# Windowed attention with one tile shape for everything but the score products, and score banks shared by two engines

## The chip, the cores and the metric

The kernel runs on one core of a Trainium2 chip. The metric is the device time of one execution in microseconds (us); the time before is the median of three runs. A change of 0.2% is about what a measurement of this kernel can tell from none.

## The reference

```python
# x: (1, 224, 224, 96), wqkv: (96, 288), wo: (96, 96), all bf16; sw = 8, C = 96, C2 = 48
qkv = einsum('bhwc,cd->bhwd', x, wqkv);  q, k, v = split(qkv, 3)
# first half of the channels: 28 horizontal stripes of 8 x 224 = 1792 tokens
ah = softmax(qh @ kh.T * C2**-0.5);   oh = ah @ vh
# second half: 28 vertical stripes of 224 x 8 = 1792 tokens
av = softmax(qv @ kv.T * C2**-0.5);   ov = av @ vv
return concat(oh, ov) @ wo
```

So there are 56 independent attention windows, each of 1792 queries by 1792 keys with 48 channels, and a projection in front and behind. Nearly all work is the scores (QK), their exponential, and the product of the exponentials with V (PV).

## The kernel before, in words

Windows go in pairs `P` = 0 to 27 (14 horizontal pairs, then 14 vertical ones); the two windows of a pair are called `w` = 0 and 1 and use partitions 0 to 63 and 64 to 127. A pair's queries are cut into four chunks `CH` of 512, 512, 512 and 256, its keys into 14 tiles of 128. A *unit* is one chunk by one key tile (two key tiles in the 256-wide chunk), for both windows: 49 units a pair, 1372 in all.

One unit's QK is two matmuls of 512 columns, one a window, with 48 rows by 128 columns of weights (four of 256 columns in the short chunk): the array is then used as two tiles of 64 rows by 128 columns, which run side by side. One unit's PV is two matmuls with 128 rows by 49 columns of weights (48 channels of V and a column of ones that sums the exponentials): two tiles of 128 rows by 64 columns, side by side again.

Units are of two sorts. `a_units` (42 a pair, 1176 in all): QK writes two PSUM banks, ScalarE takes the exponential of both in one ACTIVATE (L672) into `PT`, PV reads it. `d_units` (7 a pair, 196 in all, numbers `ND`, `NDL`): VectorE approximates the exponential as a sum of `J` = 4 terms. It scales the scores (L698, one instruction a window, `Y_sb`), makes four integer images of them (L710, `L_sb`), and TensorE adds four PVs with four scaled copies of V (`VD_sb`, made by GpSimd at L495).

Around this lie the *fills*, products that prepare the next pair and finish the last: transposes of x (L409, L422; weights of 96 columns over 112 or 128 rows), the projections to K and Q (L437; 96 rows by 64 columns, two side by side), to V (L481; 96 rows by 128 columns), and the output projection (`fin`: L519 for horizontal pairs, 49 by 64; L550 for vertical ones, 49 by 128). VectorE moves each result out of PSUM.

PSUM has eight banks. Banks 0 to 3 are two pairs (`a_sets`) for the ACTIVATEs. Banks 4 to 7 (`banks`) are shared by the score halves of `d_units`, the fills and the open PV sums (at most two, `live`).

The order of work on each engine is not written by hand. `Planner` simulates five engines with a cost per operation (`dur`) and a delay between engines (`SLACK`), and takes from a set of streams, each with a priority, what can start first; among what can start within 0.03 us, the lowest priority number. On TensorE these are `pe_qa`, `pe_qd`, `pe_pd`, `pe_pa`, `pe_fin`, `pe_fill` = 0 to 5. The result is a fixed order with semaphore waits, which every engine follows: an instruction that waits holds all behind it on that engine. `soft` dependences only pace the plan. The SyncE queue issues all DMAs.

Of the kernel before, what the change touches and what calls it, by code (L numbers as in the profile page):

```python
# [45 lines left out]
ND = 2  # L46
NDL = 1


class Op:  # L50
    __slots__ = ("eng", "dur", "fn", "deps", "soft", "alloc", "then", "idx", "end", "wait", "tok", "dma")

    def __init__(s, eng, dur, fn, deps=(), soft=(), alloc=(), then=None, dma=None):
        s.eng, s.dur, s.fn, s.deps, s.soft, s.alloc, s.then = eng, dur, fn, list(deps), list(soft), list(alloc), then
        s.idx = s.end = s.wait = None
        s.tok, s.dma = {}, dma


class Pool:
# [6 lines left out]
    def peek(s, when):  # L66
        best = None
        for k in s.slots:
            f = s.free_by[k]
            if f is None or any(o.end is None for o in f):  # L70
                continue
            t = max([when(o) for o in f], default=0.0)
            if best is None or t < best[0]:
                best = (t, k)
        return best

    def take(s, k):
        f = s.free_by[k]
        s.free_by[k] = None
        return f  # L80
# [5 lines left out]
SLACK = {  # L86
    ("act", "pe"): 0.10, ("pe", "act"): 0.15, ("dve", "pe"): 0.4, ("pe", "dve"): 0.35, ("dve", "dve"): 0.05,
    ("pool", "pe"): 1.5, ("dve", "pool"): 0.3, ("pool", "dve"): 0.8, ("pool", "pool"): 0.1, ("pe", "pe"): 0.0,
    ("dve", "sp"): 0.2, ("pool", "sp"): 0.2, ("pe", "sp"): 0.2, ("sp", "pe"): 1.0, ("sp", "dve"): 1.0,
    ("sp", "pool"): 1.0, ("act", "dve"): 0.2, ("dve", "act"): 0.2, ("act", "act"): 0.0, ("pe", "pool"): 0.3,  # L90
    ("sp", "sp"): 0.0, ("act", "sp"): 0.2,
}


class Planner:
    def __init__(s, sems):
        s.sems = sems
        s.t = {e: 0.0 for e in ("pe", "act", "dve", "pool", "sp")}
        s.n = {e: 0 for e in s.t}
        s.out = {e: [] for e in s.t}  # L100
        s.streams = {e: [] for e in s.t}
        s.dma_tot = {}

    def stream(s, eng, prio):
        q = deque()
        s.streams[eng].append((prio, q))
        return q

    def when(s, o, eng):
        return o.end + SLACK.get((o.eng, eng), 0.3)  # L110

    def ready(s, op):
        t = 0.0
        for d in op.deps + op.soft:
            if d.end is None:
                return None
            t = max(t, s.when(d, op.eng))
        for pool, _ in op.alloc:
            b = pool.peek(lambda o: s.when(o, op.eng))
            if b is None:  # L120
                return None
            t = max(t, b[0])
        return t

    def place(s, op, t):
        deps = list(op.deps)
        for pool, name in op.alloc:
            k = pool.peek(lambda o: s.when(o, op.eng))[1]
            deps += pool.take(k)
            op.tok[name] = k  # L130
        e = op.eng
        op.end = t + op.dur
        if op.dma is not None:
# [6 lines left out]
            s.t[e] = t + 0.06  # L140
        else:
# [4 lines left out]
            s.t[e] = op.end  # L146
        if op.then:
            op.then(op)

    def run(s):  # L150
        while True:
            best = None
            for e, streams in s.streams.items():
                cands = []
                for prio, q in streams:
                    if q:
                        r = s.ready(q[0])
                        if r is not None:
                            cands.append((max(r, s.t[e]), prio, q))
                if not cands:  # L160
                    continue
                m = min(c[0] for c in cands)
                c = min((c for c in cands if c[0] <= m + 0.03), key=lambda c: c[1])
# [5 lines left out]
        left = {e: [len(q) for _, q in st] for e, st in s.streams.items() if any(q for _, q in st)}  # L169
        assert not left, left  # L170


def bass_standalone__window_attn_cswin__vision_kernel(
# [11 lines left out]
    CP = C2 + 2  # L185
# [9 lines left out]
    FS, VS = 5, 10  # L195
    scale = float(C2) ** -0.5
    A128 = scale * log2(2.718281828459045) * 128.0
    DKT = max(ND, 2 * NDL)
    NPT, NY, NL = 6, 3, 3
    LEAD, SPACE = 5, 4  # L200

    es = ExitStack()
    with es:
# [3 lines left out]
        w_sb = sb("w_sb", [C, 6, 64], BF16)  # L207
        woh = sb("woh", [128, C + 1], BF16)
        wov = sb("wov", [128, C + 1], BF16)
# [6 lines left out]
        xT_sb = [sb(f"xT_sb{i}", [C, 2, NTOK], BF16) for i in range(2)]  # L216
# [3 lines left out]
        VD_sb = [sb(f"VD_sb{i}", [128, J, 2, max(DKT, 1), CP], BF16) for i in range(2)]  # L220
# [9 lines left out]
        rc = [sb(f"rc{i}", [128, FS], FP32) for i in range(4)]  # L230
        tmp = [sb(f"tmp{i}", [128, FS, C], FP32) for i in range(4)]
        ps = es.enter_context(nc.psum_tensor("ps", [128, 8 * 512], FP32))

        def bank(i):
            return ps[:, i * 512:(i + 1) * 512]

# [10 lines left out]
        pe_qa, pe_qd, pe_pd, pe_pa, pe_fin, pe_fill = (pl.stream("pe", i) for i in range(6))  # L247
# [8 lines left out]
        rcs, tmps = Pool(range(4)), Pool(range(4))  # L256

        def first(eng, dur, fn, deps=()):
            op = Op(eng, dur, fn, deps)
            q_first[eng].append(op)  # L260
            return op

# [5 lines left out]
        first("dve", 0.15, lambda e: e.memset(woh[:], 0.0))  # L268
        o_wov0 = first("dve", 0.15, lambda e: e.memset(wov[:], 0.0))
# [4 lines left out]
        o_ps0 = first("dve", 1.8, lambda e: e.memset(ps[:, 4 * 512:8 * 512], 0.0))  # L274
        for b in range(2):
            o_v1 = first("dve", 0.1, lambda e, b=b: e.memset(V_sb[b][:, :, :, C2:CP], 1.0))
        for k in banks.slots:
            banks.free(k, [o_ps0])
        for i in range(8):
            first("pe", 0.43, lambda e, i=i: e.matmul(bank(i % 4)[:, :], lhsT=warm[:, 0:128], rhs=warm[:, :],  # L280
                                                      start=True, stop=True), [o_warm])
# [9 lines left out]
        def load(P, stream):  # L291
            b = P % 2
            for w in range(2):
                src = x_flat[(2 * P + w) * NTOK:(2 * P + w + 1) * NTOK, :].rearrange("(k p) c -> p k c", p=TH) if is_h[P] else None
                for hf in range(2):
# [7 lines left out]
                    for i, (dst, s_) in enumerate(todo):  # L303
                        op = Op("sp", 2.5, lambda e, dst=dst, s_=s_: e.dma_start(dst, s_),  # L304
# [6 lines left out]
        op_w0 = Op("sp", 2.5, lambda e: e.dma_start(w_sb[:, :, 0:C2], wqkv.rearrange("c (s d) -> c s d", s=6)), [o_w0], dma=(s_w0, 0))  # L311
        q_first["sp"].insert(1, op_w0)
        load(1, q_first["sp"])
        for dst, r0 in ((woh, 0), (wov, C2)):
            for p0 in (0, 64):
                op_w = Op("sp", 2.5, lambda e, dst=dst, r0=r0, p0=p0: e.dma_start(dst[p0:p0 + C2, 0:C], wo[r0:r0 + C2, :]),
                          [o_wov0], dma=(s_w, 0))
                q_first["sp"].append(op_w)
        for dst in (woh, wov):
            for p0 in (C2, 64 + C2):  # L320
                op_w = Op("sp", 2.5, lambda e, dst=dst, p0=p0: e.dma_start(dst[p0:p0 + 1, C:C + 1], one_sb[0:1, 0:1]),
                          [o_one], dma=(s_w, 0))
                q_first["sp"].append(op_w)
# [33 lines left out]

# [3 lines left out]
        def fill(pe_dur, pe_fn, pe_deps, evs, soft=(), stream=None):  # L361

            def freed(op):
                banks.free(p.tok["b"], [op])
            p = Op("pe", pe_dur, lambda e: pe_fn(e, bank(p.tok["b"])), pe_deps, soft, [(banks, "b")])
            ops = []
            prev = p
            for k, (eng, dur, fn, deps, reads, st, alloc, then) in enumerate(evs):
                op = Op(eng, dur, None, [prev] + list(deps), [], alloc)
                op.fn = lambda e, fn=fn, op=op: fn(e, bank(p.tok["b"]), op)  # L370
                ops.append(op)
                op.then = then
# [4 lines left out]
            def both(op):  # L377
                freed(op)
# [11 lines left out]
        def prep(P, pace=None, startup=False):  # L390
# [12 lines left out]
            for w in range(2):  # L403
                for hf in range(2):
                    if is_h[P]:
                        def pe_fn(e, bk, w=w, hf=hf):
                            bkb = bk.bitcast(BF16)
                            for j in range(FTH):
                                ins = e.transpose(bkb[0:C, j * TH:(j + 1) * TH], x_sb[b][0:TH, w, hf * FTH + j, :], ident[0:TH, 0:TH])  # L409
                            return ins  # L410

                        def ev_fn(e, bk, op, w=w, hf=hf):
                            src = bk.bitcast(BF16)[0:C, 0:FTH * TH].rearrange("c (r bc dw) -> c r bc dw", r=RPF, dw=8)
                            dst = xT_sb[b][:, w, :].rearrange("c (bc r dw) -> c r bc dw", r=SW, dw=8)[:, hf * RPF:(hf + 1) * RPF, :, :]
                            return e.tensor_copy(dst, src)  # L415
                    else:
                        ks = list(range(8 * hf, min(NKT, 8 * hf + 8)))

                        def pe_fn(e, bk, w=w, ks=ks):
                            bkb = bk.bitcast(BF16)  # L420
                            for j, k in enumerate(ks):
                                ins = e.transpose(bkb[0:C, j * 128:(j + 1) * 128], x_sb[b][:, w, k, :], ident[:])  # L422
                            return ins

                        def ev_fn(e, bk, op, w=w, ks=ks):
                            return e.tensor_copy(xT_sb[b][:, w, ks[0] * 128:(ks[-1] + 1) * 128], bk.bitcast(BF16)[0:C, 0:len(ks) * 128])  # L426
                    p, ops = fill(0.65, pe_fn, [x_op[(P, w, hf)], o_ident],
                                  [("dve", 0.62, ev_fn, xt_war, True, dve_ev, [], None)], soft() + xt_war)
# [4 lines left out]
            for kind in "kq":  # L433
                for c, (q0, qs) in enumerate(CH):
# [5 lines left out]
                    if kind == "q":  # L440
# [4 lines left out]
                        else:  # L445
                            def ev_fn(e, bk, op, q0=q0, qs=qs):
                                return e.tensor_copy(QT_sb[b][:, q0:q0 + qs], bk[:, 0:qs])  # L447
                            evs = [("dve", 0.63, ev_fn, qk_war, True, dve_ev, [], None)]
                    else:
# [3 lines left out]
                        evs = [("dve", 0.72, ev_fn, qk_war, True, dve_ev, [], None)]  # L453
                        if c == NCH - 1:
# [359 lines left out]
```

## Time and profile before

| | |
|---|---|
| median of 3 runs | 1202.9 us (1201.15 to 1203.32) |
| span of the profiled execution | 1199.9 us |
| TensorE, matmuls (PE) | 1177.9 us busy, 10872 matmuls |
| VectorE (DVE) | 980.0 us busy |
| ScalarE (ACT) | 1135.3 us busy |
| GpSimd (POOL) | 195.4 us busy |
| granted TensorE clock | 0.995 over the span |

The profiled execution's own time is not listed apart from its span; the span runs from its first to its last instruction, 3.0 us below the median of the runs. PE is the row of matmuls and PEld that of weight loads, which overlap them. The ends of matmuls are modelled, so PE's busy share tells little; the distance from start to start tells more. A group "x2352 | 460.2, 386 | 9.6" has 2352 instructions, 460.2 us in which at least one ran, 386 ns for one, and 9.6 us in which the engine stood idle just before one. The chain that ended last, read in order of time, gives for each stretch of one line on TensorE the time until the next stretch starts.

### The profile page before, as it was taken

The page shows a single profiled execution, that of the slowest core. Times are in us where ns is not written, and L with a number is a line of the kernel's source. Part 1 is how long each engine was busy: PE and PEld are TensorE (multiplying, and loading weights), DVE is VectorE, ACT ScalarE, POOL GpSimd, SP SyncE. Part 2 cuts the span into 40 slices and gives each one's busy share as a digit, 9 for nine tenths or more (in the row PEclk, how much of TensorE's full clock was granted, in tenths as well). Part 3 has the DMA queues.
Part 4 walks back from the last instruction along what each step waited for, and adds up shares of the span by engine and source line. Part 5 has one row for each costly group of instructions (what it writes and reads, how often), then busy time and mean ns, then how long its engine had stood idle before and what let it go on. Part 6 is the DMA issues. An engine that isn't in the chain of part 4 may idle for free.

```text
span 1199.9 us, 26677 instructions
## 1 busy us (share of the span) xinstructions
PE 1177.9 (98%) x10872; PEld 441.8 (37%) x10872; DVE 980.0 (82%) x2331; ACT 1135.3 (95%) x1182; POOL 195.4 (16%) x256
## 2 busy tenths in 40 slices
PE   8999999999999999999999999999999999999996
PEld 3333333333333333333333333333333333333332
DVE  7877887888888788788789888887888888888884
ACT  6999999999999999999999999999999999999997
POOL 0100100110010010011003212222222232222221
PEclk8999999999999999999999999999999999999998
DMA  3110110011011001001002211111211221121001
GB/s 73 25 24 1 24 25 18 7 24 24 2 24 24 11 15 24 10 16 25 15 12 37 38 33 35 31 29 36 36 33 34 37 36 33 34 38 21 18 18 24
DMA packets 164946, 30.74 MB, mean 26 GB/s; under 512 B 164824, under 2 KB 164824, under 8 KB 164824
## 3 DMA queue, kind: packets, MB, share of 16 engines
q1 hardware_dynamic: 164824, 29.05, 13.2%
q8 instruction: 85, 1.39, 0.5%
q14 instruction: 37, 0.30, 0.1%
HBM read 19.36 MB, written 9.63 MB: 24 GB/s over the span
## 4 chain that ended last, share of the span: by engine, by line
PE 88%; ACT 10%; DVE 1%; DMA 0%; issue 0%; SPq 0%; ACTq 0%; POOL 0%; POOLq 0%
PE ps L636 43%; PE ps L658 32%; ACT PT L672 10%; PE ps L481 2%; PE ps L422 2%; PE ps L409 2%; PE ps L437 2%; PE ps L519 2%; PE ps L550 2%; DMA x_sb<-in_x_dram 0%; DVE L_sb L710 0%; ACT QT_sb L443 0%; DVE Y_sb L698 0%; SPq L304 0%; DVE OT_sb L597 0%
## 5 line engine op out<-in xcount | busy, mean ns | idle before, releaser
L672 ACT ACTIVATE PT<-ps 128x1024 bf16<-128x1024 f32 x1176 | 1131.8, 1032 | 47.4 <-PE ps L658 28.8
L658 PE MATMUL ps<-QT_sb,KT_sb 48*128 48x512 bf16 (+1 forms) x3136 | 523.7, 358 | 10.0 <-ACT PT L672 8.8
L636 PE MATMUL ps<-PT,V_sb 128*49 128x512 bf16 (+1 forms) x2688 | 435.4, 364 | 0.7 <-ACT PT L672 0.7
L710 DVE TENSOR_SCALAR L_sb<-Y_sb 128x1024 int16<-128x1024 f16 x784 | 326.2, 447 | 1.7
L698 DVE TENSOR_SCALAR Y_sb<-ps 128x512 f16<-128x512 f32 x392 | 257.5, 685 | 66.5 <-PE ps L658 62.2
L636 PE MATMUL ps<-L_sb,VD_sb 128*49 128x512 bf16 (+1 forms) x1792 | 274.4, 361 | 0.5 <-DVE L_sb L710 0.5
L658 PEld LDWEIGHTS ps<-QT_sb,KT_sb 48*128 48x128 bf16 x3136 | 136.4, 93 | 320.5 <-issue 157.0
L636 PEld LDWEIGHTS ps<-PT,V_sb 128*49 128x49 bf16 x2688 | 126.8, 103 | 202.7 <-issue 181.1
L564 POOL TENSOR_TENSOR out_sb<-tmp,Ph_sb 128x384 bf16<-128x384 f32 (+1 forms) x112 | 100.2, 907 | 368.6 <-DVE rc L556 198.2
L636 PEld LDWEIGHTS ps<-L_sb,VD_sb 128*49 128x49 bf16 x1792 | 79.4, 103 | 115.0 <-issue 43.7
L462 POOL TENSOR_SCALAR KT_sb<-KT_sb,negmean 128x1792 bf16<-128x1792 bf16 x27 | 48.8, 1808 | 429.8 <-DVE kjunk L456 250.6
L597 DVE CAST OT_sb<-ps 113x512 bf16<-113x512 f32 x112 | 69.5, 621 | 13.9 <-PE ps L636 10.2
L495 POOL TENSOR_SCALAR VD_sb<-V_sb 128x200 bf16<-128x200 bf16 x112 | 46.0, 411 | 199.9 <-DVE V_sb L486 193.2
L451 DVE TENSOR_SCALAR_CACHE_REDUCE KT_sb<-ps 128x512 bf16<-128x512 f32 x112 | 67.9, 620 | 8.9 <-PE ps L437 7.0
L437 PE MATMUL ps<-xT_sb,w_sb 96*64 96x512 bf16 x448 | 72.3, 354 | 1.3 <-DVE xT_sb L415 0.7
L447 DVE CAST QT_sb<-ps 128x512 bf16<-128x512 f32 x108 | 64.4, 618 | 9.4 <-PE ps L437 8.3
L486 DVE CAST V_sb<-ps 128x480 bf16<-128x480 f32 x112 | 56.0, 502 | 8.0 <-PE ps L481 7.9
L415 DVE COPY xT_sb<-ps 96x896 bf16<-96x896 bf16 x56 | 34.7, 620 | 28.1 <-PE ps L409 27.0
L560 DVE TENSOR_TENSOR tmp<-ps,rc 128x384 f32<-128x384 f32 (+1 forms) x112 | 55.9, 499 | 0.7
L529 DVE TENSOR_TENSOR Ph_sb<-ps,rc 128x384 bf16<-128x384 f32 x98 | 53.9, 550 | 0.7
L426 DVE COPY xT_sb<-ps 96x1024 bf16<-96x1024 bf16 (+1 forms) x56 | 34.4, 615 | 18.2 <-PE ps L422 17.8
L525 DVE RECIPROCAL rc<-ps 128x4 f32<-128x4 f32 x98 | 17.3, 177 | 36.3 <-PE ps L519 35.3
(35 smaller groups left out, 353.5 us busy)
## 6 DMA issues: line engine op xcount, KB each, us to landing
x_sb<-in_x_dram SPq DMA_DIRECT2D x56, 168.0 KB, 3.4
x_sb<-in_x_dram SPq DMA_DIRECT2D x392, 24.0 KB, 2.2
out_dram<-out_sb SPq DMA_DIRECT2D x392, 24.0 KB, 1.9
w_sb<-in_wqkv_dram SPq DMA_DIRECT2D x1, 54.0 KB, 2.8
woh<-in_wo_dram SPq DMA_DIRECT2D x2, 9.0 KB
wov<-in_wo_dram SPq DMA_DIRECT2D x2, 9.0 KB
woh<-one_sb SPq DMA_DIRECT2D x2, 0.0 KB
wov<-one_sb SPq DMA_DIRECT2D x2, 0.0 KB
```

The source lines that it names most:

```text
L437: ins = e.matmul(bk[64 * w:64 * w + 64, 0:qs], lhsT=w_sb[:, wblk(P, kind), :], rhs=xT_sb[b][:, w, q0:q0 + qs], start=True, stop=True)
L447: return e.tensor_copy(QT_sb[b][:, q0:q0 + qs], bk[:, 0:qs])
L451: return e.tensor_scalar(KT_sb[b][:, q0:q0 + qs], bk[:, 0:qs], 1.0, None, ALU.mult, ALU.add, accum_out=ksum[b][:, c:c + 1])
L486: return e.tensor_copy(V_sb[b][:, w, k0:k0 + n, 0:C2], bk[:, 0:n * C2].rearrange("p (j c) -> p j c", j=n))
L560: return e.tensor_tensor(tmp[op.tok["t"]][:, 0:n, :], bk[:, 0:n * (C + 1)].rearrange("p (s c) -> p s c", s=n)[:, :, 0:C], r[:, 0:n].unsque ...
L564: return e.tensor_tensor(out_sb[b][:, w, g[0]:g[0] + n, :], tmp[hold[1].tok["t"]][:, 0:n, :], Ph_sb[:, g[0]:g[0] + n, j, :], ALU.add)
L597: return e.tensor_copy(OT_sb[b][0:64 + CA, q0:q0 + qs], bk[0:64 + CA, 0:qs])
L636: ins = e.matmul(bank(k.bank)[64 * w:64 * w + CA, 0:qs], lhsT=lhs(w, kt), rhs=rhs(w, i, qs), start=(op.tok["first"] and i == 0), stop=(k.l ...
L658: ins = e.matmul(dst[w][:, i * qs:(i + 1) * qs], lhsT=KT_sb[b][64 * w:64 * w + C2, kt * 128:(kt + 1) * 128], rhs=QT_sb[b][64 * w:64 * w + ...
L672: a.fn = lambda e: e.activation(PT[a.tok["p"]][:], ps[:, 1024 * q.tok["s"]:1024 * q.tok["s"] + 1024], ACTF.Exp, scale=scale)
L698: d.fn = lambda e, w=w, q=q: e.tensor_scalar(Y_sb[hold["y"].tok["y"]][:, w * 512:(w + 1) * 512], bank(q.tok["b"])[:, :], A128, Y_MIN, ALU. ...
L710: t.fn = lambda e, j=j: e.tensor_scalar(L_sb[hold["l"].tok["l"]][:, j, :], Y_sb[hold["y"].tok["y"]][:, :], 127.0 * 128.0 + 128.0 * SPL_S[j ...
```

## The change

Five things are done together.

1. **Tile shapes.** All matmuls but QK are given weights of 128 rows by 64 columns. V and its scaled copies are padded to 64 columns (`CP` = 64). The transposes become two matmuls each, for channels 0 to 63 and 32 to 95, the V projection and the vertical output projection two of 64 tokens each; the output weights become four tensors with zeros in the other window's rows.
2. **Banks.** Banks 0 to 5 are three pairs (`ring`) shared by `a_units`, `d_units` and, half a pair at a time, fills (`FillPool`); at most one pair is in the fills' hands. Banks 6 and 7 (`obanks`) hold the open PV sums, and a fill where exactly one sum is open and not near its end.
3. **`d_units`** write a pair, and VectorE scales both banks in one instruction of 1024 elements.
4. **The planner** has an occupancy and a latency per operation, tighter delays between engines, and for TensorE a rule of its own (`pick_pe`): it counts `SWITCH` = 0.10 us for a change between shape "q" (QK) and "v" (all else), stays in "v" until two pairs are free (`BATCH`) or ScalarE is about to run out, and stays in "q" while a QK is ready or soon will be.
5. **Small ones.** Eight `PT` buffers for six and two `Y_sb` for three, other priorities, the PSUM memset gone, the input weights loaded in two DMAs.

```diff
-ND = 2
-NDL = 1
+NDC = [2, 2, 2, 1]
+DKT = 2
...
-SLACK = {
-    ("act", "pe"): 0.10, ("pe", "act"): 0.15, ("dve", "pe"): 0.4, ("pe", "dve"): 0.35, ("dve", "dve"): 0.05,
...
+LINK = {("dve", "dve"): 0.035, ("pe", "pe"): -9.0, ("pool", "dve"): 0.1, ("pool", "pe"): 0.3, ("pool", "pool"): 0.1,
+        ("act", "pe"): 0.055, ("sp", "pe"): 0.5, ("sp", "dve"): 0.5, ("sp", "pool"): 0.5}
+SWITCH = 0.10
...
+    def n_q(s, t):
+        return sum(1 for w, _ in s.ring.order(lambda o: s.when(o, "pe")) if w <= t + EPS)
+
+    def pick_pe(s, cands):
+        t = s.t["pe"]
+        run_end = max(s.t["act"], t) + 0.903 * s.pend
+        C = []
+        for r, prio, q in cands:
+            C.append((max(r, t + (SWITCH if q[0].mode != s.mode else 0.0)), prio, q))
+        if any(c[1] == PRIO[0] for c in C) and run_end - t < DRUN:
+            C = [c for c in C if c[1] != PRIO[1]]
+        V = [c for c in C if c[2][0].mode == "v"]
+        Q = [c for c in C if c[2][0].mode == "q"]
+        now = t + EPS
+        first = min(C, key=lambda c: (c[0], c[1]))
+        if s.mode == "q":
+            q_now = [c for c in Q if c[0] <= now]
+            if q_now:
+                return min(q_now, key=lambda c: c[1])
+            v_now = [c for c in V if c[0] <= now + SWITCH]
+            q_soon = [c for c in Q if c[0] <= t + HOLD]
+            if q_soon:
+                return min(q_soon, key=lambda c: c[0])
+            if v_now:
+                return min(v_now, key=lambda c: c[1])
+            return first
+        v_now = [c for c in V if c[0] <= now]
+        q_now = [c for c in Q if c[0] <= t + SWITCH + EPS]
+        need = SWITCH + 0.46
+        if v_now:
+            c = min(v_now, key=lambda c: c[1])
+            if q_now:
+                if t + c[2][0].occ > run_end - need:
+                    return min(q_now, key=lambda c: c[1])
+                if t > run_end - RUN and s.n_q(t + SWITCH) >= BATCH:
+                    return min(q_now, key=lambda c: c[1])
+            return c
+        if q_now and (s.n_q(t + SWITCH) >= BATCH or t + 0.25 > run_end - need):
+            return min(q_now, key=lambda c: c[1])
+        return first
...
+EPS, HOLD, RUN, BATCH = 0.02, 0.12, 1.5, 2
+PRIO = (1, 0, 3, 5, 4, 2)
+NEAR, LEAD, SPACE, PACE, DRUN = 1, 3, 4, 0.9, 0.9
...
-    CP = C2 + 2
+    CP = 64
-    NPT, NY, NL = 6, 3, 3
-    LEAD, SPACE = 5, 4
+    NPT, NY, NL, NR = 8, 2, 3, 4
...
-        banks = Pool([4, 5, 6, 7])
-        a_sets = Pool([0, 1])
+        ring = Pool([0, 1, 2])
+        obanks = Pool([6, 7])
+        class FillPool:
...
+            def peek(s, when, n):
+                near = any(k.left <= NEAR for k in live) or len(live) != 1
+                got = obanks.order(when)
+                if got and not near:
+                    return (got[0][0], [got[0][1]])
+                opt = []
+                for k, f in s.half.items():
+                    if f is not None and all(o.end is not None for o in f):
+                        opt.append((max([when(o) for o in f], default=0.0), k))
+                if s.pair is None:
+                    opt += [(t, 2 * p) for t, p in ring.order(when)]
+                opt.sort()
+                opt = opt or got
+                return (opt[0][0], [opt[0][1]]) if opt else None
...
-        o_ps0 = first("dve", 1.8, lambda e: e.memset(ps[:, 4 * 512:8 * 512], 0.0))
...
-        op_w0 = Op("sp", 2.5, lambda e: e.dma_start(w_sb[:, :, 0:C2], wqkv.rearrange("c (s d) -> c s d", s=6)), [o_w0], dma=(s_w0, 0))
+        op_w0 = Op("sp", 0.7, 2.8, lambda e: e.dma_start(w_sb[0:64, :, 0:C2], wqkv.rearrange("c (s d) -> c s d", s=6)[0:64]), [o_w0], dma=(s_w0, 0))
         q_first["sp"].insert(1, op_w0)
+        op_w0 = Op("sp", 0.7, 2.8, lambda e: e.dma_start(w_sb[96:128, :, 0:C2], wqkv.rearrange("c (s d) -> c s d", s=6)[64:96]), [o_w0], dma=(s_w0, 0))
+        q_first["sp"].insert(2, op_w0)
...
-                                ins = e.transpose(bkb[0:C, j * 128:(j + 1) * 128], x_sb[b][:, w, k, :], ident[:])
+                            for h in range(2):
+                                ins = e.transpose(bkb[64 * h:64 * h + 64, j * tp:(j + 1) * tp], x_sb[b][0:tp, w, k, 32 * h:32 * h + 64],
+                                                  ident[0:tp, 0:tp])
...
-                            ins = e.matmul(bk[:, j * C2:(j + 1) * C2], lhsT=xT_sb[b][:, w, (k0 + j) * 128:(k0 + j + 1) * 128],
-                                           rhs=w_sb[:, wblk(P, "v"), 0:C2], start=True, stop=True)
+                            for h in range(2):
+                                t0 = (k0 + j) * 128 + 64 * h
+                                ins = e.matmul(bk[64 * h:64 * h + 64, j * C2:(j + 1) * C2], lhsT=xT_sb[b][:, w, t0:t0 + 64],
+                                               rhs=w_sb[:, wblk(P, "v"), 0:C2], start=True, stop=True)
...
-                                ins = e.matmul(bk3[64 * w:64 * w + 64, s, :], lhsT=OT_sb[b][64 * w:64 * w + CA, bc * 64:(bc + 1) * 64],
-                                               rhs=woh[64 * w:64 * w + CA, :], start=True, stop=True)
+                                ins = e.matmul(bk3[64 * w:64 * w + 64, s, :], lhsT=OT_sb[b][:, bc * 64:(bc + 1) * 64],
+                                               rhs=wo_sb[0][w][:, :], start=True, stop=True)
...
-            a = Op("act", 0.918, None, [q], [], [(pts, "p")], act_then)
-            a.fn = lambda e: e.activation(PT[a.tok["p"]][:], ps[:, 1024 * q.tok["s"]:1024 * q.tok["s"] + 1024], ACTF.Exp, scale=scale)
+            a = Op("act", 0.903, 1.023, None, [q], [], [(pts, "p", 1)], act_then)
+            a.fn = lambda e: e.activation(PT[a.tok["p"]][:].rearrange("p (s n) -> p s n", s=2), two(q.tok["s"]), ACTF.Exp, scale=scale)
...
-                q = Op("pe", 0.12, None, [k_ready[P], q_ready[(P, c)]], soft, [(banks, "b")])
-                d = Op("dve", 0.63, None, [q], [], [(ys, "y")] if w == 0 else [])
+            q = Op("pe", 0.222, 0.40, None, [k_ready[P], q_ready[(P, c)]], soft, [(ring, "s", 1)], mode="q")
+            d = Op("dve", 1.13, 1.22, None, [q], [], [(ys, "y", 1)], d_then)
```

More of the change, by code (lines that the diff above doesn't have):

```diff
@@ L64, in __init__, with order @@
         s.free_by = {k: [] for k in s.slots}
-    def peek(s, when):
-        best = None
+    def order(s, when):
+        got = []
         for k in s.slots:
@@ L102, in __init__, with stream @@
         s.dma_tot = {}
-    def stream(s, eng, prio):
+        s.mode = "v"
+        s.pend = 0
+        s.switches = 0
+        s.busy = {e: 0.0 for e in s.t}
+    def stream(s, eng, prio, mode=None):
         q = deque()
@@ L126, in place @@
         deps = list(op.deps)
[L127 to L130, printed above, removed]
+        for pool, name, n in op.alloc:
+            ks = pool.peek(lambda o: s.when(o, op.eng), n)[1]
+            deps += pool.take(ks)
+            op.tok[name] = ks[0] if n == 1 else sorted(ks)
         e = op.eng
-        op.end = t + op.dur
+        op.start, op.end = t, t + op.lat
+        s.busy[e] += op.occ
+        if e == "pe":
+            if op.mode != s.mode:
+                s.switches += 1
+            s.mode = op.mode
         if op.dma is not None:
@@ L205, in sb @@
             return es.enter_context(nc.sbuf_tensor(name, shape, dt))
-        w_sb = sb("w_sb", [C, 6, 64], BF16)
-        woh = sb("woh", [128, C + 1], BF16)
-        wov = sb("wov", [128, C + 1], BF16)
+        w_sb = sb("w_sb", [128, 6, 64], BF16)
+        wo_sb = [[sb(f"wo_sb{v}{w}", [128, C + 1], BF16) for w in range(2)] for v in range(2)]
         ident = sb("ident", [128, 128], BF16)
@@ L267, in bass_standalone__window_attn_cswin__vision_kernel @@
         o_w0 = first("dve", 0.25, lambda e: e.memset(w_sb[:], 0.0))
-        first("dve", 0.15, lambda e: e.memset(woh[:], 0.0))
-        o_wov0 = first("dve", 0.15, lambda e: e.memset(wov[:], 0.0))
+        for v in range(2):
+            for w in range(2):
+                o_wov0 = first("dve", 0.15, lambda e, v=v, w=w: e.memset(wo_sb[v][w][:], 0.0))
         o_one = first("dve", 0.1, lambda e: e.memset(one_sb[:], 1.0))
@@ L377, in both @@
             def both(op):
-                freed(op)
+                fills.free(p.tok["b"], [op])
                 if old:
@@ L596, in evac @@
             def evac(e):
-                return e.tensor_copy(OT_sb[b][0:64 + CA, q0:q0 + qs], bk[0:64 + CA, 0:qs])
+                return e.tensor_copy(OT_sb[b][:, q0:q0 + qs], bk[:, 0:qs])
             def then(ev):
-                banks.free(k.bank, [ev])
+                obanks.free(k.bank, [ev])
                 live.remove(k)
@@ L741, in bass_standalone__window_attn_cswin__vision_kernel @@
                 base = a_start[P]
-                prep(P + 1, pace=lambda n, base=base: [act_of[base + int(n * NA * 0.8 / NFILL)]])
+                prep(P + 1, pace=lambda n, base=base: [act_of[base + int(n * NA * PACE / 16)]])
         pl.run()
+        import os
+        if os.environ.get("PLAN"):
+            print("plan", {e: round(v, 1) for e, v in pl.t.items()}, "busy", {e: round(v, 1) for e, v in pl.busy.items()}, "sw", pl.switches)
         def emit(eng, name):
```

317 lines of the change are left out of this document (172 added, 145 removed).

## The prediction

> **What bounds the kernel now.** I read the page first, then the chain that ended last in order of time, then the timeline of single engines.
>
> ```profile
> span 1199.9 us, 26677 instructions
> PE 1177.9 (98%) x10872; PEld 441.8 (37%) x10872; DVE 980.0 (82%) x2331; ACT 1135.3 (95%) x1182; POOL 195.4 (16%) x256
> ...
> PE 88%; ACT 10%; DVE 1%; DMA 0%; issue 0%; SPq 0%; ACTq 0%; POOL 0%; POOLq 0%
> ...
> L672 ACT ACTIVATE PT<-ps 128x1024 bf16<-128x1024 f32 x1176 | 1131.8, 1032 | 47.4 <-PE ps L658 28.8
> ```
>
> TensorE and ScalarE both look full, but the chain lies on TensorE for 88%. The chain in detail says what TensorE spends:
>
> ```profile
> 601.60 0.33 PE ps L636 x2
> 601.93 0.35 PE ps L481 x10
> ...
> 611.43 0.29 PE ps L519 x8
> ...
> 614.40 0.58 PE ps L422 x8
> 614.98 0.32 PE ps L658 x2
> 615.30 0.55 PE ps L636 x4
> 615.85 0.32 PE ps L658 x2
> 616.17 0.76 PE ps L636 x6
> 616.94 0.54 PE ps L658 x4
> 617.47 0.55 PE ps L636 x4
> ```
>
> One QK pair costs 0.32 us and two cost 0.54; one PV pair 0.33, two 0.55, three 0.76. So a pair costs 0.22 and each stretch about 0.10 to 0.12 more. That extra is the price of leaving a tile shape, not of leaving a line:
>
> ```profile
> 671.69 0.40 PE L636 MATMUL ps<-PT,V_sb 128*49 128x512 bf16 x2
> 672.02 0.39 PE L658 MATMUL ps<-QT_sb,KT_sb 48*128 48x512 bf16 x2
> 672.34 0.40 PE L636 MATMUL ps<-PT,V_sb 128*49 128x512 bf16 x2
> 672.58 0.39 PE L437 MATMUL ps<-xT_sb,w_sb 96*64 96x512 bf16 x2
> 672.89 0.39 PE L658 MATMUL ps<-QT_sb,KT_sb 48*128 48x512 bf16 x2
> ```
>
> From PV to QK the starts are 0.33 apart, from PV to the K projection (also 128 rows by 64 columns) 0.24. Taken from start to start over the whole trace, the median surcharge is 0.104 from QK to PV and 0.119 back, together 0.223 for a **round**. Counting rounds over the trace, by tile shape in order of start, gives 1145 stretches of 64-by-128 tiles, the first and last at
>
> ```profile
> 12.31 1.24 PE L658 MATMUL ps<-QT_sb,KT_sb 48*128 48x512 bf16 x6
> ...
> 1189.52 0.39 PE L658 MATMUL ps<-QT_sb,KT_sb 48*128 48x256 bf16 x4 [0.19 <-ACT PT L672]
> ```
>
> so almost one for each of the 1176 ACTIVATEs: 1145 x 0.223 = 255 us. The fills with other shapes come in
>
> ```profile
> L486 DVE CAST V_sb<-ps 128x480 bf16<-128x480 f32 x112 | 56.0, 502 | 8.0 <-PE ps L481 7.9
> L415 DVE COPY xT_sb<-ps 96x896 bf16<-96x896 bf16 x56 | 34.7, 620 | 28.1 <-PE ps L409 27.0
> ...
> L426 DVE COPY xT_sb<-ps 96x1024 bf16<-96x1024 bf16 (+1 forms) x56 | 34.4, 615 | 18.2 <-PE ps L422 17.8
> ...
> L525 DVE RECIPROCAL rc<-ps 128x4 f32<-128x4 f32 x98 | 17.3, 177 | 36.3 <-PE ps L519 35.3
> ```
>
> 112 + 56 + 56 + 98 = 322 groups, of which some adjoin: 285 stretches. Each is a detour of one more change, at a mean 0.113 (half of 0.223, and the same within 0.01 in the trace): 32 us. So 287 us of TensorE's time are changes of shape; beside them about 40 us are waits and the start.
>
> The second limit is ScalarE:
>
> ```profile
> 12.74 3.77 ACT L672 ACTIVATE PT<-ps 128x1024 bf16<-128x1024 f32 x4 [0.69 <-PE ps L658]
> ...
> 1130.87 11.11 ACT L672 ACTIVATE PT<-ps 128x1024 bf16<-128x1024 f32 x12 [0.31 <-PE ps L658]
> ...
> 1164.83 26.47 ACT L672 ACTIVATE PT<-ps 128x1024 bf16<-128x1024 f32 x28 [0.27 <-PE ps L658]
> ```
>
> When it is fed without a break, twelve take 11.11 us with 1.02 for the last: (11.11 - 1.02) / 11 = 0.917 each. 1176 of them take 1078 us, where the stretch from 12.74 to 1164.83 + 26.47 = 1191.30 takes 1178.6. ScalarE thus loses 100 us to TensorE. Ahead of it lie 12.7 us, behind it 8.6.
>
> **The change, part by part.**
>
> *Fewer shapes.* The detours go: their groups get the shape of PV and join a stretch of it. Minus 285 x 0.113 = 32 us, all of it on TensorE's path. I bound what could remain at 0 to 5 us.
>
> *Fewer rounds.* The new order stays in one shape until two score pairs are free. How many rounds R are left? The ends are 686 (all 1372 QKs go two by two) and 1145 (as now). Three pairs allow two by two when all three serve ScalarE: one is being read, one waits, and when the next ACTIVATE starts two are free with 1.8 us of ScalarE's work ahead less the time gone. A `d_unit` takes a pair away. VectorE's rows:
>
> ```profile
> L698 DVE TENSOR_SCALAR Y_sb<-ps 128x512 f16<-128x512 f32 x392 | 257.5, 685 | 66.5 <-PE ps L658 62.2
> ```
>
> and in the timeline
>
> ```profile
> 600.00 1.34 DVE L698 TENSOR_SCALAR Y_sb<-ps 128x512 f16<-128x512 f32 x2 [0.33 <-PE ps L658]
> ```
>
> With 0.39 for the QK, some 1.3 for the scaling and 0.3 of waiting (the wait in the row) it is held for 2.0 us, in each stretch of 1176 / 196 = 6 ACTIVATEs or 5.5 us. In those two ACTIVATE times QKs go one by one (two rounds); the other four take two rounds, and the `d_unit`'s own QK rides along: 4 x 196 = 784. Fills take half a pair only while two PV sums are open or the one is nearly closed; I put that at 12 of the 38 us per window pair (four turnovers of 3 us), a third of the 28 x 23.5 = 658 fill groups, about 220 of some 1.3 us, two at a time at best: 150 to 200 us in which one pair is missing, and so about 50 rounds more. R = 830 lies nearer the low end because the row of the `d_unit` fixes most of it. (1145 - 830) x 0.223 = minus 70 us, between 0 and minus 102.
>
> *More matmuls in the fills.* 392 + 448 transposes become pairs side by side:
>
> ```profile
> L481 PE MATMUL ps<-w_sb,xT_sb 96*128 96x48 bf16 x784 | 35.8, 184 | 0.1
> L409 PE MATMUL ps<-ident,x_sb 112*96 112x112 bf16 x448 | 34.5, 223 | 0.2 <-DMA x_sb<-in_x_dram 0.2
> L422 PE MATMUL ps<-ident,x_sb 128*96 128x128 bf16 x392 | 33.1, 224 | 0.0
> L519 PE MATMUL ps<-woh,OT_sb 49*64 49x97 bf16 x784 | 32.7, 208 | 0.0
> L550 PE MATMUL ps<-wov,OT_sb 49*128 49x97 bf16 x392 | 29.6, 206 | 0.6 <-DVE OT_sb L597 0.5
> ```
>
> Eight take 0.58 less 0.11, 0.058 each, long enough for two issues: no change. The V projection's ten take 0.35 less 0.10, 0.025 each with 48 columns streamed, which is not the stream's time but one matmul's issue. Twice the matmuls at 0.025: 784 x 0.025 = plus 20 us; none if two tiles cost what one did. L519 keeps its count (0.29 less 0.10 for eight, 0.024 each). L550 doubles to 784, at 0.024 each and with two side by side before in part: plus 0 to 9, I take 3. Sum plus 23, from 0 to 29. That holds if weights load in the shade, as they do in the same shape today:
>
> ```profile
> 1185.23 0.57 PEld L636 LDWEIGHTS ps<-L_sb,VD_sb 128*49 128x49 bf16 x12 [0.21 <-DVE L_sb L710]
> 1185.23 0.84 PE L636 MATMUL ps<-L_sb,VD_sb 128*49 128x256 bf16 x12
> ```
>
> Twelve loads fit in 0.57 us while six pairs of 256 columns stream at 0.11 a pair. For 48 and 97 columns in this shape no row of before can tell; the last rival below prices loads that are not hidden. The Trainium skill, *TensorE: Matmul & The Clock Gate*, Part 3, has it that a weight load overlaps a running matmul only where the row group differs, which in tiles of 128 rows it never does; the two rows above disagree.
>
> *Padding* V to 64 columns and contracting over 128 rows changes no streamed column: L437, which has 64 columns, streams at the pace of PV with 49. Nothing on the path. GpSimd's copies L495 grow from 200 to 256 elements, at most by the same ratio; GpSimd is 16% busy and works a window pair ahead.
>
> *One scaling instruction* in place of two frees VectorE 0 to 0.15 us a unit (0.68 + 0.61 today), 0 to 29 us in all, off the path; but whatever stands behind it in VectorE's order waits up to 1.3 us instead of 0.69, and a fill's bank comes free that much later. I take nothing, and carry the loss in the second rival.
>
> *ScalarE's read* of two banks as two rows of 512 has the same elements as the row shown: 0, with 10 ns in either direction worth 12 us.
>
> *Start and end.* The second DMA for the input weights goes into SyncE's queue ahead of all x loads but the first, at one issue time:
>
> ```profile
> 1.40 0.75 SPq L311 DMA_DIRECT2D w_sb<-in_wqkv_dram  x1
> ```
>
> Plus 0.7 us on the first ACTIVATE, which waits for x. The PSUM memset ended at 3.9 us, before x landed at 7.1: its loss gives nothing. The end is as before.
>
> *Sum* against the profiled execution: 1199.9 + 0.7 - 32 - 70 + 23 = 1121.6 us of span, with waits as today. The median of the runs stood 3.0 above the span: **1125 us**, minus 6.5%.
>
> What is late next is ScalarE: 12.7 + 0.7 + 1078 + 8.6 = 1100 of span, 1103 as a median. No plan can go below that with 1176 ACTIVATEs. The planner counts 0.903 an ACTIVATE against the 0.917 above, 16 us over the run, so its order will find ScalarE later than planned.
>
> **The rivals.**
>
> *ScalarE becomes the whole bound.* If R is under about 750, TensorE needs less than ScalarE and the time is the floor with a few waits: 1103 to 1108. For it: 1.8 us of work queued per two QKs. Against: the `d_units` take the third pair for over a third of the time.
>
> *The shared pairs starve ScalarE* (the other side). Banks 4 to 7 today absorb every late VectorE operation; VectorE is 82% busy and serves both `d_units` and fills. If a fill's half pair and a `d_unit`'s pair are out together, ScalarE has one pair: its step becomes 0.92 + 0.1 + 0.39 + 0.1 = 1.5 us, 0.6 more, and TensorE, in a fixed order, waits as well. The gain of 78 us is gone when 130 ACTIVATEs, 11%, go so. At 17%, 200 of them, the time is 1125 + 120 = 1245. For it: margins between engines in the plan are thin. Against: only one pair may be with the fills, and a third of fills at most need it.
>
> *The batches don't form* (the change doesn't do what it says): R stays near 1145, and only the detours go: 1199.9 + 0.7 - 32 + 23 + 3 = 1195. Half-formed batches lie between 1150 and 1195.
>
> *Weight loads in the open* in the small 128-by-64 matmuls: 840 + 784 + 784 pairs, each with 0.105 (a load in the rows of L636) instead of today's 0.058, 0.025 and 0.048 a pair or single, plus the stream: about 240 us more, 1340. Against: the twelve loads above. By the rule of the Trainium skill (*TensorE: Matmul & The Clock Gate*, Part 3) this is what would come.
>
> **How the numbers follow.** Forecast, R from 750 to 940: 0.60 (1108 to 1150). ScalarE the whole bound: 0.15. Batches half formed or not: 0.13 (1150 to 1195, in which 0.02 reads as no change within 0.2%, about what a measurement of this kernel can tell). Starved: 0.09, of which 0.08 slower than before. Loads in the open: 0.03. The range must reach the ScalarE floor, 1102, and into the half-formed batches, 1172; above it lies some 0.16, below it 0.03. Faster: 0.60 + 0.15 + 0.11 + 0.01 = 0.87; same 0.02; slower 0.11.
>
> **What would show it.** Right: the detours gone; QK stretches of four matmuls as the commonest, about 830 of them; PV and V projection following each other at 0.22 to 0.24; the ACTIVATEs at 0.917 for long stretches and idle before them well under 47 us; V projection at about 0.05 a token tile. Wrong: QK stretches still of two matmuls; waits of TensorE for L698's successor or a fill's evacuation of several tenths, in hundreds; a start-to-start of small matmuls near 0.1. The weakest step is R, which no row of before shows.

## The result and the profile after

1149.5 us (median of 4 runs, 1147.3 to 1150.8) after 1202.8: ratio 0.956, interval 0.954 to 0.958. The forecast was 1125, the range 1102 to 1172: the sign is right and the time lies in the range, but a third of the gain is missing.

The page of the changed kernel (QK is now L762, PV L745, the ACTIVATE L780, the scaling L804, the terms L814):

```profile
span 1149.0 us, 30551 instructions
...
PE 1109.8 (97%) x12888; PEld 459.3 (40%) x12888; DVE 977.8 (85%) x2138; ACT 1094.7 (95%) x1182; POOL 198.3 (17%) x256
...
PE 53%; DVE 25%; ACT 19%; issue 2%; DMA 0%; SPq 0%; ACTq 0%; POOL 0%; POOLq 0%
...
L780 ACT ACTIVATE PT<-ps 128x1024 bf16<-128x1024 f32 x1176 | 1091.2, 1085 | 36.1 <-PE ps L762 26.1
...
L814 DVE TENSOR_SCALAR L_sb<-Y_sb 128x1024 int16<-128x1024 f16 x784 | 351.1, 486 | 0.7
L804 DVE TENSOR_SCALAR Y_sb<-ps 128x1024 f16<-128x1024 f32 x196 | 239.2, 1221 | 60.2 <-PE ps L762 58.2
```

VectorE has come into the chain that ended last: 25%, where it had 1%. And an instruction that the change doesn't touch has become longer, a term of the exponential. In the page before its row was

```profile
L710 DVE TENSOR_SCALAR L_sb<-Y_sb 128x1024 int16<-128x1024 f16 x784 | 326.2, 447 | 1.7
```

The chain of the changed kernel in order of time (start, us until the next stretch starts, stretch) answers to the one shown of before:

```profile
603.43 0.34 PE ps L597 x20
...
616.27 0.54 PE ps L762 x4
616.80 0.34 PE ps L745 x2
617.14 0.32 PE ps L762 x2
617.46 0.57 PE ps L538 x16
...
620.77 0.22 PE ps L551 x2
620.99 0.22 PE ps L745 x2
621.20 0.17 PE ps L666 x8
621.38 0.43 PE ps L745 x4
```

The K projection (L551) and PV now follow each other at the bare price of a pair, 0.22, the output projection's eight (L666) take 0.17, and the surcharge of about 0.10 stands only around QK. Twenty small matmuls of the V projection (L597) take 0.34; before, ten took 0.35, of which 0.10 was for the change of shape.

To see where the time went I set up an account of TensorE for each kernel, from its first to its last matmul: the *stream* (each matmul's columns at full clock, or, for the small ones, the spacing seen in their stretches), the *changes of shape* at 0.1115 us (their number is counted in the trace, the mean is half of the 0.223 of before), and the *rest*, which is waiting and the start.

| | stream | changes of shape | rest | QK stretches |
|---|---|---|---|---|
| before | 861.9 | 2564: 285.9 | 43.4 | 1145 |
| after | 863.1 | 1767: 197.0 | 80.8 | 883 |
| difference | +1.2 | -88.9 | +37.4 | |

By this account the changes of shape gave 89 us, and 37 were given back, most of it as waits. It is softer than its digits in three places:

- *The price of a change.* In the trace of before, the next pair starts 0.319 after a QK pair of 512 columns and 0.315 after a PV pair where the shape changes (medians), and 0.216 where it doesn't (lower quartile). So a change costs nearer 0.10 than 0.1115; the column of changes may be up to a tenth too high, and the rest too low by as much.
- *The stream.* The pairs of the V projection start 0.032 apart, the single ones of before 0.025: 784 times 0.007 is 5 us, not 1.
- *The clock at the start.* The granted clock from 10 to 15, 15 to 20 and 20 to 25 us was 0.50, 0.50 and 0.79 in this profile and 0.77, 0.54 and 1.00 in that of before. By my estimate from these numbers this costs TensorE some 6 and some 3.5 us of full clock, so 2 to 3 of the 37 are no waits.

### The profile page after: what moved, and what is told of

Read it like the earlier page. It is cut to its first block, busy times and chain, and to the rows that moved or that the text cites. A ratio compares the mean times of both kernels' runs of the same rounds, so it can differ in the third digit from the quotient of the medians.

```text
span 1149.0 us, 30551 instructions
## 1 busy us (share of the span) xinstructions
PE 1109.8 (97%) x12888; PEld 459.3 (40%) x12888; DVE 977.8 (85%) x2138; ACT 1094.7 (95%) x1182; POOL 198.3 (17%) x256
## 4 chain that ended last, share of the span: by engine, by line
PE 53%; DVE 25%; ACT 19%; issue 2%; DMA 0%; SPq 0%; ACTq 0%; POOL 0%; POOLq 0%
PE ps L745 24%; PE ps L762 19%; ACT PT L780 19%; DVE L_sb L814 10%; DVE Y_sb L804 7%; PE ps L538 4%; PE ps L551 3%; DVE OT_sb L709 2%; DVE KT_sb L565 2%; DVE tmp L673 2%; PE ps L597 2%; PE ps L637 1%; DVE QT_sb L561 1%; DVE V_sb L602 1%; PE ps L666 1%
## 5 line engine op out<-in xcount | busy, mean ns | idle before, releaser
L780 ACT ACTIVATE PT<-ps 128x1024 bf16<-128x1024 f32 x1176 | 1091.2, 1085 | 36.1 <-PE ps L762 26.1
L762 PE MATMUL ps<-QT_sb,KT_sb 48*128 48x512 bf16 (+1 forms) x3136 | 458.2, 357 | 8.5 <-DVE V_sb L602 1.7
L745 PE MATMUL ps<-PT,V_sb 128*64 128x512 bf16 (+1 forms) x2688 | 388.3, 360 | 0.7 <-ACT PT L780 0.7
L814 DVE TENSOR_SCALAR L_sb<-Y_sb 128x1024 int16<-128x1024 f16 x784 | 351.1, 486 | 0.7
L804 DVE TENSOR_SCALAR Y_sb<-ps 128x1024 f16<-128x1024 f32 x196 | 239.2, 1221 | 60.2 <-PE ps L762 58.2
L745 PE MATMUL ps<-L_sb,VD_sb 128*64 128x512 bf16 (+1 forms) x1792 | 270.8, 363 | 18.0 <-DVE L_sb L814 15.1
L762 PEld LDWEIGHTS ps<-QT_sb,KT_sb 48*128 48x128 bf16 x3136 | 122.0, 93 | 292.9 <-ACT PT L780 175.5
L745 PEld LDWEIGHTS ps<-PT,V_sb 128*64 128x64 bf16 x2688 | 126.9, 109 | 127.0 <-issue 104.0
L745 PEld LDWEIGHTS ps<-L_sb,VD_sb 128*64 128x64 bf16 x1792 | 85.5, 108 | 135.8 <-DVE L_sb L814 75.5
L610 POOL TENSOR_SCALAR VD_sb<-V_sb 128x256 bf16<-128x256 bf16 x112 | 51.4, 459 | 261.3 <-DVE V_sb L602 254.6
L709 DVE CAST OT_sb<-ps 128x512 bf16<-128x512 f32 x112 | 69.0, 616 | 28.7 <-PE ps L745 28.5
L551 PE MATMUL ps<-xT_sb,w_sb 128*64 128x512 bf16 x448 | 81.3, 374 | 1.1 <-DVE xT_sb L526 0.7
L538 PE MATMUL ps<-ident,x_sb 112*64 112x112 bf16 (+1 forms) x1680 | 63.3, 219 | 2.4 <-DMA x_sb<-in_x_dram 1.1
```

Source lines behind the costliest of these rows:

```text
L538: ins = e.transpose(bkb[64 * h:64 * h + 64, j * tp:(j + 1) * tp], x_sb[b][0:tp, w, k, 32 * h:32 * h + 64], ident[0:tp, 0:tp])
L551: ins = e.matmul(bk[64 * w:64 * w + 64, 0:qs], lhsT=w_sb[:, wblk(P, kind), :], rhs=xT_sb[b][:, w, q0:q0 + qs], start=True, stop=True)
L709: return e.tensor_copy(OT_sb[b][:, q0:q0 + qs], bk[:, 0:qs])
L745: ins = e.matmul(bank(k.bank)[64 * w:64 * w + 64, 0:qs], lhsT=lhs(w, kt), rhs=rhs(w, i, qs), start=(op.tok["first"] and i == 0), stop=(k.l ...
L762: ins = e.matmul(bank(2 * s + w)[:, i * qs:(i + 1) * qs], lhsT=KT_sb[b][64 * w:64 * w + C2, kt * 128:(kt + 1) * 128], rhs=QT_sb[b][64 * w: ...
L780: a.fn = lambda e: e.activation(PT[a.tok["p"]][:].rearrange("p (s n) -> p s n", s=2), two(q.tok["s"]), ACTF.Exp, scale=scale)
```

## The experiments

The theory after the comparison: the terms L814 are held up by GpSimd. Split by what GpSimd does meanwhile, a term takes 0.416 us on the mean beside nothing (580 of 784), 0.55 beside a scaled copy of V (96), 0.73 beside an output sum (65), 0.91 beside the subtraction of K's mean (43). (Each term is counted with the GpSimd instruction that it overlaps most; eight meet two of them, so other ways of counting give other means for the last two, as in the first expectation below.) TensorE has a fixed order, and in the account 25 us of its waits end with a term's end, where before it was 0.8. TensorE hardly waits for GpSimd's own results: in its rows of waits these come to 0.2 us. The rivals: margins between engines that are too thin whoever is late, the shared pairs of banks, and a floor by ScalarE.

The timeline shows one such case in the changed kernel, VectorE first, then GpSimd, TensorE and ScalarE:

```profile
1080.09 1.95 DVE L814 TENSOR_SCALAR L_sb<-Y_sb 128x1024 int16<-128x1024 f16 x2
...
1079.67 1.76 POOL L576 TENSOR_SCALAR KT_sb<-KT_sb,negmean 128x1792 bf16<-128x1792 bf16 x1 [6.31 <-DVE kjunk L570]
...
1080.35 0.51 PE L666 MATMUL ps<-wo_sb,OT_sb 128*64 128x97 bf16 x16
1081.76 0.41 PE L745 MATMUL ps<-L_sb,VD_sb 128*64 128x512 bf16 x2 [0.90 <-DVE L_sb L814]
...
1082.75 1.02 ACT L780 ACTIVATE PT<-ps 128x1024 bf16<-128x1024 f32 x1 [0.64 <-PE ps L762]
```

Two terms take 1.95 us: the first alone takes 1.62 and ends 0.28 after GpSimd's instruction (1079.67 + 1.76); TensorE stands 0.90 us before the PV that reads the term, though PVs and QKs of other units stand behind it; ScalarE runs dry for 0.64. This is the rule and not one case: all 22 terms that start while a subtraction of K's mean runs end 0.28 us after it, whether that makes them 0.92 or 1.62 long. Those that started before it take 0.39 to 0.42, and then the subtraction is the longer one, 1.92 to 2.12 for 1.76.

**GpSimd's work cut to slivers.** The same order; left out are most of the subtraction of K's mean, of the scaled copies and of the output sums.

```diff
-  KT_sb[b][:, :] + negmean                  (1792 columns)
+  KT_sb[b][:, 0:8] + negmean
-  VD_sb[b][:, j, :, :, :] = V * SPL_W[j]    (64 channels)
+  VD_sb[b][:, j, :, :, 0:2] = ...
-  out_sb[..., :] = tmp + Ph                 (96 channels)
+  out_sb[..., 0:2] = ...                    # rest zeroed once at the start
```

> The changed kernel in its own order, with GpSimd's three repeated instructions cut to a few elements each: K's mean is subtracted from 8 columns only, the scaled V copies hold 2 of 64 channels, the output sum is formed for 2 of 96 channels (the rest is zero). In the changed kernel a term of the exponential (L814) takes 0.416 us where GpSimd is idle, but 0.55, 0.75 and 0.78 on the mean beside its three instructions, and TensorE loses some 25 us right after such terms. Theory (GpSimd holds VectorE up and TensorE's fixed order waits for it): the terms come back to 0.42 on the mean, the loss after them falls under 5 us, and the time to 1120 to 1130. Rival (the order's margins are too thin for any engine, and GpSimd is chance): 1142 to 1150, with the loss moved to other VectorE operations. Second rival (the shared pairs are what costs): no less than 1145.

Measured: 1116.8 us, ratio to before 0.930 (0.928 to 0.931). The same pair of terms in this kernel, and TensorE beside it:

```profile
1048.09 0.75 DVE L818 TENSOR_SCALAR L_sb<-Y_sb 128x1024 int16<-128x1024 f16 x2
...
1048.37 0.51 PE L670 MATMUL ps<-wo_sb,OT_sb 128*64 128x97 bf16 x16
1048.71 0.38 PE L749 MATMUL ps<-L_sb,VD_sb 128*64 128x512 bf16 x2
```

0.75 for 1.95, and no wait before the PV. Over the whole kernel:

```profile
span 1114.7 us, 30556 instructions
...
ACT 65%; PE 33%; DVE 1%; DMA 0%; issue 0%; SPq 0%; ACTq 0%; POOLq 0%; POOL 0%
...
L818 DVE TENSOR_SCALAR L_sb<-Y_sb 128x1024 int16<-128x1024 f16 x784 | 297.1, 418 | 0.7
```

The terms are back at 0.418 on the mean, VectorE is out of the chain, which now lies on ScalarE for 65%. QK stretches are 883 as in the changed kernel, the rest falls from 80.8 to 47.1, and of the waits behind terms about 1 us is left. With the same order, margins and pairs and as many ACTIVATEs, none of the three rivals can be the main cause. It gained a little more (33 us) than I expected at most. Some of that is the clock at the start, which was 1.00 throughout in this profile: the two executions with a mean granted clock of 0.998, 1147.3 and 1116.5, lie 31 us apart.

**The same in the kernel before.** The identical cut in the old kernel and its old order.

> The kernel before, in its own order, with GpSimd's three repeated instructions cut to a few elements as in e1 (the same parts of the computation left out). Theory (GpSimd held VectorE up before the change too, but TensorE's changes of shape hid it): the terms fall from 0.447 to 0.42 us and the time stays within 4 us of 1202.8, so that the cost came out only when TensorE got faster. Rival (the hold cost before as it does after): 1170 to 1185.

Measured: 1200.8, ratio 0.998 (0.997 to 0.9995), with the terms shorter:

```profile
span 1201.1 us, 26682 instructions
...
L714 DVE TENSOR_SCALAR L_sb<-Y_sb 128x1024 int16<-128x1024 f16 x784 | 300.3, 415 | 1.7
```

GpSimd held VectorE up before too, for 26 us of the terms' busy time (326.2 to 300.3), and it cost about 2 us. My reading is that TensorE, late anyway by its changes of shape, was the cover, and that the change took it away; the run without batches below bears that out, but no run shows it by itself.

**An order that minds GpSimd.** The planner gets one resource more.

```diff
+        if op.port:                      # GpSimd's instructions and the terms
+            t = max(t, s.port)           # in ready()
...
+        if op.port:
+            s.port = t + op.occ          # in place()
...
-        run_end = max(s.t["act"], t) + 0.903 * s.pend
+        run_end = max(s.t["act"], t) + 0.917 * s.pend
-            a = Op("act", 0.903, 1.023, ...
+            a = Op("act", 0.917, 1.06, ...
```

GpSimd's copies of V are also counted 0.1 us longer (0.456 for 0.356, the trace has 0.459).

> The changed kernel with a planner that lets no GpSimd instruction run beside a term of the exponential, and counts 0.917 us an ACTIVATE instead of 0.903. The instructions are the same, their order differs. Theory (GpSimd holds VectorE up): the terms fall to 0.42 to 0.45 us, TensorE's loss after them under 10 us, time 1118 to 1132. Rival (thin margins): 1143 to 1155, as the order is no looser. Rival (ScalarE is already the bound): no lower than 1140.

Measured: 1120.2, ratio 0.932 (0.930 to 0.933), within the theory's range:

```profile
L820 DVE TENSOR_SCALAR L_sb<-Y_sb 128x1024 int16<-128x1024 f16 x784 | 321.7, 450 | 0.8
```

The terms came down half of the way only (0.450; I expected 0.45 at most), and of TensorE's waits behind them 10 us stayed (I expected less than 10).

**Its two edits apart.** First the port alone (with the longer copies of V), then the cost of an ACTIVATE alone.

> Of e2's two edits the first alone: the planner keeps GpSimd's instructions and the terms of the exponential (L814) apart, and still counts 0.903 us an ACTIVATE. Theory (keeping them apart is what gained): 1118 to 1130, terms at 0.42 to 0.46 us. Rival (counting ScalarE rightly gained): 1140 to 1152.

> Of e2's two edits the second alone: the planner counts 0.917 us an ACTIVATE and lets GpSimd run beside the terms. Theory (keeping them apart is what gained): 1138 to 1152, terms at 0.47 to 0.50 us, TensorE's loss after them 18 us or more. Rival (counting ScalarE rightly gained): 1115 to 1128.

Measured: 1126.3 (0.937, 0.935 to 0.938) and 1136.2 (0.945, 0.943 to 0.946). The port does most of it, with terms at 0.432. The second came out 2 us under the theory's range and 13 us below the changed kernel, with terms at 0.469 and 23 us still lost behind them: part of the gain is order as such.

**Two controls**, each the changed kernel with one number of the planner moved, GpSimd not minded: `LEAD` = 4 for 3, `HOLD` = 0.10 for 0.12.

> A control: the changed kernel with LEAD = 4 for 3, which asks for d_units one ACTIVATE earlier and so gives another order, with GpSimd not minded. Theory (GpSimd's hold costs some 25 us in any order that doesn't mind it): 1138 to 1158, the terms at 0.46 us or more. Rival (the changed kernel's order is an unlucky one, and any other would do): 1115 to 1132.

> A second control: the changed kernel with HOLD = 0.10 for 0.12, another order again, with GpSimd not minded. Theory: 1138 to 1158, the terms at 0.46 us or more. Rival (an unlucky order): 1115 to 1132.

Measured: 1137.1 (0.945, 0.944 to 0.947), terms at 0.454, just under both numbers I gave, and 1145.6 (0.953, 0.951 to 0.954), terms at 0.475. Orders that don't mind GpSimd spread over 1136 to 1150 (the run with wide margins, below, among them), with the changed kernel at the top, and those that do lie at 1116 to 1126 (the last two runs among them). So by my estimate some 8 of the 33 us are the bad luck of one order (1149.5 against 1141, the mean of the other four).

**Wide margins.** `LINK` from VectorE to TensorE 0.345 for 0.045.

> The changed kernel with a margin of 0.345 us for 0.045 between an end on VectorE and a start on TensorE in the plan, GpSimd not minded. Rounds rise, as the plan holds the pairs longer: 946 for 883, 14 us. Theory (GpSimd's hold, up to 1.6 us at a time, is what TensorE waits for): the margin covers a third of it, 8 us of 25, and the time is 1148 to 1162. Rival (thin margins): the waits go, 1120 to 1138.

Measured: 1145.9 (0.953, 0.952 to 0.955), 2 us under the theory's range, far from the rival's. The rest fell by 19 us to 62.0, but QK stretches rose to 946 as foreseen and took 14 back. (Up to 6 of the 19 may be the clock at the start, which was not halved in this profile.) The waits behind terms fell by about two thirds, where I had expected a third. Margins cover such waits and cost nearly as much.

**The tile shapes alone**, in the kernel before with its own banks, planner and costs: the matmuls of the diff with 128 by 64, padded V, four output weights.

> The kernel before with the tile shapes of the change alone: its own banks, planner, costs and pairs of score instructions. Theory (285 detours at 0.113 us go, and the added matmuls cost 1 us): minus 31 us, 1166 to 1178, with 1140 to 1180 stretches of QK shape. Rival (added matmuls cost the 23 us of the prediction): 1190 to 1196. Rival (the shape counts for nothing without the order): 1200 or more.

Measured: 1174.9, ratio 0.977 (0.976 to 0.979). Changes of shape fell from 285.9 to 258.3 us, the stream rose by 1.2, the rest stayed at 42.2. The first theory holds; the added matmuls cost a few us at most.

**No batches.** `BATCH` = 1 for 2 in the changed kernel.

> The changed kernel with BATCH = 1: TensorE leaves the PV shape as soon as one pair is free. Theory (a round costs 0.223 us and rounds decide): QK stretches rise from 883 to between 1040 and 1100, 35 to 48 us more for changes of shape, of which waits give back some 10: 1172 to 1188. Rival (ScalarE or VectorE sets the time and rounds are hidden): 1145 to 1158.

Measured: 1170.7, ratio 0.974 (0.972 to 0.975), 1.3 us under the range given. QK stretches 1052, changes of shape 234.7 us, 38 more; the rest gave back 17. The waits behind terms fell to about half, with the terms still at 0.462: there is more cover again.

**GpSimd relieved.** On top of the order that minds it: the scaled copies on VectorE, and then K's mean there too (with `PACE` = 0.85).

```diff
-                op = Op("pool", 0.2 + ..., 0.25 + ..., lambda e, j=j: e.tensor_scalar(
+                op = Op("dve", 0.14, 0.21, lambda e, j=j: e.tensor_scalar(
...
-                pool_v.append(op)
+                dve_vd.append(op)        # a stream of its own, priority 2
```

> e2 with the scaled copies of V made by VectorE in place of GpSimd (112 instructions of 128x256 elements, some 0.14 us each, 16 us more for VectorE). Theory (GpSimd holds VectorE up): in e2 the terms beside these copies still took 0.55 us for 0.42, 82 of them, 11 us of VectorE, so the terms fall to 0.43 on the mean; VectorE has 15% to spare; 1110 to 1120. Rival (VectorE's own load counts more than GpSimd's hold): 1121 to 1130.

> e7 with K's mean subtracted on VectorE too (27 instructions of 128x1792, some 0.69 us each by the one at the start, 18 us more for VectorE), and PACE = 0.85. GpSimd keeps the output sums alone. Theory (GpSimd's hold): the terms at 0.42 us and the time 1108 to 1116, as the floor by ScalarE is some 1103. Rival (VectorE's load): 1118 to 1128.

Measured: **1116.0** (0.928, 0.927 to 0.929) and 1121.2 (0.932, 0.931 to 0.934). The first is the best version, faster than the kernels before and after the change:

```profile
span 1114.5 us, 30507 instructions
...
ACT 58%; PE 34%; DVE 6%; issue 1%; DMA 0%; SPq 0%; ACTq 0%; POOL 0%; POOLq 0%
...
L821 DVE TENSOR_SCALAR L_sb<-Y_sb 128x1024 int16<-128x1024 f16 x784 | 305.9, 427 | 0.8
```

Its chain lies on ScalarE, 13 us above the 1103 that I gave as ScalarE's floor. The second missed the theory's range and lies in that of the rival, VectorE's load: its terms are at 0.438, no shorter than the first's 0.427, its QK stretches rose to 916, and VectorE has 24 us more to do. The order and the pace changed with it, so which of these costs the 5 us stays open.

## Why the prediction was right or wrong

- *What bounds the kernel*: right. A third of what the changes of shape had cost, 89 of 286 us, was to be had: 28 us by the shapes alone, 38 between no batches and batches of two, and the other 24 came with the new banks and planner.
- *Detours, minus 32*: right; the account has no stretch of another shape left after the start, and the shapes alone gave 28.
- *Rounds, R = 830, minus 70*: 883, minus 58. A term mis-sized by 12 us (with 0.20 for a round, as read again above, 262 rounds are 53 us and it is 17): 399 stretches of one QK and 479 of two, where the forecast had fewer singles. Whether it was the `d_units` or the fills that took the third pair was not tried.
- *More matmuls, plus 23*: plus 1 in the account, plus 5 by the starts. The step that failed is twice the matmuls at 0.025, "one matmul's issue": in tiles side by side two of 48 columns together take 0.032, little more than one did, near the lower bound of the term. Weight loads in the open, the last rival, is out:

```profile
603.25 0.39 PEld L597 LDWEIGHTS ps<-w_sb,xT_sb 128*64 128x64 bf16 x20 [0.30 <-DVE tmp L673]
603.26 0.49 PE L597 MATMUL ps<-w_sb,xT_sb 128*64 128x48 bf16 x20
```

Twenty loads start and end within 0.39 us beside their matmuls, in tiles of all 128 rows, and the twenty matmuls start within 0.30 us, where the rival had 0.105 for each pair. The rule in the Trainium skill, *TensorE: Matmul & The Clock Gate*, Part 3, that a load overlaps a running matmul only where the row group differs, does not hold here.
- *Waits as today, 0*: this is the step that made the forecast too low, by 37 us. "GpSimd is 16% busy" was read as harmless. The row of the terms had the sign in it: a mean of 447 ns, where those in the timeline mostly take 410 to 420, and I did not ask what the long ones stood beside. The start took 2 of the 37, with the clock that was lower there: the first ACTIVATE came at 14.9 us in this execution and at 12.7 before; in other kernels' profiles, that with the old order among them, it moves by 2 us too.
- *The starved pairs*: not what happened. In the account TensorE's waits that end with an ACTIVATE are 16 us, 20 before, and cutting GpSimd's work, with the pairs as they are, took the rest to 47.
- *ScalarE late next*: right. Where the waits are gone the chain lies mostly on ScalarE (65% and 58%), at 1116 to 1117, against a floor of 1103.
- *The sum*: in luck. The 22 us too many for matmuls hid more than half of the 37 of waits: 1121.6 + 12 - 22 + 37 is the span of 1149. With the matmuls rightly sized the forecast would have been near 1103, and the miss 46 us.

## What to carry to other kernels

Count what TensorE pays at the borders between tile shapes, start to start, and give the small work the shape of the large. Before a bound is lifted, list what it covers: a neighbour's spread in one line's durations, harmless while TensorE was late anyway, is the next cost. An order fixed by a planner must know each resource that two engines share, or the plan is off just where it is tight.

## What the runs showed of the hardware

A term on VectorE (128x1024, 16-bit from SBUF to SBUF, two back to back in 0.75 us) and a GpSimd instruction on SBUF don't run side by side; the one that comes second is held. Beside the subtraction of K's mean a term took up to 1.62 us, and with GpSimd cut to slivers 0.434 at most:

```profile
L814 DVE TENSOR_SCALAR L_sb<-Y_sb x784: 386/418/1621, 18.4 to 1135.4; 128x1024 int16<-128x1024 f16 x196
```

```profile
L818 DVE TENSOR_SCALAR L_sb<-Y_sb x784: 390/419/434, 16.9 to 1101.8; 128x1024 int16<-128x1024 f16 x196
```

(duration least, median, most in ns; the first of the changed kernel, the second of the sliver kernel). The subtraction took 1.76 us, and 1.92 to 2.12 where terms had started before it. The scaling L804, which reads PSUM, took 1.22 us beside GpSimd or not. The Trainium skill, *SBUF — State Buffer*, "Who interferes with whom", says that VectorE's two-port modes and GpSimd share a pair of ports, and whoever comes first has it for the whole instruction; the trace agrees.

Two matmuls of 48 columns in neighbouring 64-column tiles start 0.032 us before the next two; one with 128 columns of weights took 0.025.
